# First mixture layer in column chunks across batches, and a global attention product with its operands swapped

## The chip, the cores and the metric

The kernel runs on one core of one Trainium2 chip. The metric is the device time of one execution in microseconds (us): the median over runs, on the same chip, of the kernel before and the kernel after the change.

## The reference, cut to what matters

Three layers follow each other. The first is attention over a global part of 32 positions and a local part of 512 positions, with a window of 32 on each side; its 544 positions by 512 features per batch are the input of a gated layer with a convolution over three positions, and this feeds a second layer that mixes each position with the one before it.

```python
# attention, 4 batches, 8 heads of 64
out_g = softmax(scale * q_g @ k_all.T) @ v_all          # 32 global rows, all 544 columns
out_l = softmax(window of q_l @ k_l.T, and k_g) @ v
x = concat(out_g, out_l)                                # (4, 544, 512)
# first MoE
h = relu(x @ w_in)                                      # 512 -> 1024
conv = sum(conv_w[k] * shifted(h, k - 1) for k in 0, 1, 2)   # zero at both ends of a batch
x = (h * sigmoid(conv)) @ w_out                         # 1024 -> 512
# second MoE
xk = mu_k * x + (1 - mu_k) * x_prev;  xr = mu_r * x + (1 - mu_r) * x_prev
out = sigmoid(xr @ w_r) * (relu(xk @ w_k) ** 2 @ w_v)
```

## The kernel before, in words

Everything is built by a planner. `add` declares a task with an engine, a cost and buffers, and `Plan.schedule` chooses an order from costs, keys (due times) and a set of numbers at the top of the file; the instructions then stand on each engine's queue in that fixed order. Engines wait for each other by semaphores, so a late input holds everything that is queued behind it on its engine.

The attention works on 16 units, each a pair of heads of one batch (`attend`), and every second unit closes with the global rows of two units (`glob`). A unit's steps on PE (TensorE) are the scores `s`, two transposes `pe`, the products with v `o`, and a transpose `X`, which brings the result into columns. The global rows have the scores `sg`, transposes `peg`, and the value product `Xg` (`fpv`, L719), in which v is the stationary operand (64 columns) and 32 columns of probabilities stream. DVE (VectorE) masks and divides, ACT (ScalarE) exponentiates and copies. POOL (GpSimd) helps with both.

Every product of the two MoE layers is taken as three matmuls: high part by high part, high by low, low by high. The parts are made by a copy (`fh`) and a subtraction (`fl`). The first MoE (`dense`) runs batch by batch. `ph` is the product with w_in (L901) over 8 tiles of 128 features, `po` the product with w_out (L1002) over 4 tiles. The 544 positions of a batch are cut at 256 (`SPLIT`), so each weight tile is loaded for a matmul of 256 and for one of 288 columns. Between them `relu`, the convolution `c` (L936, L943), the sigmoid, the gate product (L952) and its high and low parts (`gh`, `gl`, L959, L964) run on ACT, DVE and POOL. The result goes to DRAM as `x2d`, one tile per batch.

The second MoE (`moe2`) reads `x2d` in chunks of 384, 384, 384, 512 and 512 positions. A chunk has the products `pk` (L1140, 8 tiles, weight stationary), `pr` (L1204) and `pv` (L1241). Per `pk` tile there follow a relu, a square (`sq`, L1161), a high part and a low part (`k2l`, L1173), on ACT, DVE and POOL. The weights arrive as 64-bit numbers and are narrowed on ACT, DVE and POOL; their high and low parts are made at L839 and L842.

Of the kernel before, what the change touches and what calls it, by code (L numbers as in the profile page):

```python
# [26 lines left out]
SPLIT = (0, 256, S)  # L27
SP1 = S + 1
TOK = B * S
CH = 512  # L30
# [17 lines left out]
XB = 8  # L48
T_START = 3024
STEP0 = 2060  # L50
T_DENSE = 158430
SLOT = 122790
LEAD = 618
GAP = 13519
GAP1 = 18152
STEPS_H = 6
E_BUFS = 4
H_FRAC = 0.271
LAG_TE = -1744
LAG_PV = 112946  # L60
LAG_G = 3584
# [5 lines left out]
LAG_TX = 69395  # L67
WINDOW = 108
FILL_MIN = 5374
FILL_MARGIN = 1592  # L70
FILL_START = 6
FILL_RATE = 0.834
PENALTY = 4
AHEAD = 2243
PHASES = (111983, 150041, 327818, 468472)
# [30 lines left out]
def first_col(f):  # L106

    return 32 * (f + f // 3)

# [238 lines left out]
ROWS = {"s": 128, "pv": 64, "te": 8, "tx": 8, "gt": 6, "gs": 16, "gpv": 96, "warm": 6}  # L348
# [52 lines left out]
def attn_moe_kernel(  # L401
# [26 lines left out]
    def skewed(ap):  # L428
# [6 lines left out]
        [dram.tile([P, SP1], F32, tag=f"x2d{b}_{m}", name=f"x2d{b}_{m}") for m in range(KT)]  # L435
        for b in range(B)
# [17 lines left out]
    ident = const.tile([P, P], F32, name="ident")  # L454
    mask = const.tile([P, 4, P], F32, name="mask")
# [5 lines left out]
    make_identity(nc, ident)  # L461
    nc.gpsimd.memset(mask, 0.0)

# [58 lines left out]
    def attend(u):  # L522
# [89 lines left out]
        bx = bufs["x", u]  # L612

        def fh(copy):
            copy(bx[0].tile[:, SG:], bX.tile)

        def fl():
            nc.vector.tensor_sub(bx[1].tile[:, SG:], bX.tile, bx[0].tile[:, SG:].bitcast(F32))

        h = add("ACT", act(512), lambda: fh(nc.scalar.copy), deps=[tx, ev["xa", u]],  # L620
                use=[bX] + bx, name=f"xh{u}",
                alts=[("DVE", 600, lambda: fh(nc.vector.tensor_copy))])
        l = add("DVE", tt(512), fl, deps=[h], use=[bX] + bx, name=f"xl{u}")
        ev["x", u] += [h, l]

    def x_alloc(u):
        bufs["x", u] = [buf("x0"), buf("x1")]

        def fn():
            for i, b in enumerate(bufs["x", u]):  # L630
                alloc(b, [P, S], F32R, f"x{i}_{u}")

        ev["xa", u] = add("-", 0, fn, take=bufs["x", u], name=f"xa{u}")
        ev["x", u] = []
# [5 lines left out]
    def glob(u):  # L640
# [70 lines left out]
        def fpv():  # L711
            X = alloc(bt[2], [P, 2, SG], F32, f"Xg{u}")
            eT = bT.tile
            for z in range(2):
                v = bufs["v", u - 1 + z].tile
                for n, (_, f, rows) in enumerate(gchunks):
                    for a in range(2):
                        c = SG * (2 * z + a)
# [14 lines left out]
        for q in range(2):  # L733
# [4 lines left out]
        pvd = add("PE", 1522, fpv, deps=evs + [ev["v", u - 1], ev["v", u], ev["xa", u - 1], ev["xa", u]], take=[bt[2]],  # L738
                  use=[bT, bufs["v", u - 1], bufs["v", u]], key=kt + 2000, name=f"gpv{u}")
        for z in range(2):  # L740
            uu = u - 1 + z
            bx = bufs["x", uu]

            def fh(uu=uu, z=z, bx=bx):
                nc.scalar.copy(bx[0].tile[:, 0:SG], bt[2].tile[:, z])

            def fl(z=z, bx=bx):
                nc.vector.tensor_sub(
                    bx[1].tile[:, 0:SG], bt[2].tile[:, z], bx[0].tile[:, 0:SG].bitcast(F32)
                )  # L750

            hh = add("ACT", 78, fh, deps=[pvd, ev["xa", uu]], use=[bt[2]] + bx, name=f"gxh{uu}")
            ll = add("DVE", 102, fl, deps=[hh], use=[bt[2]] + bx, name=f"gxl{uu}")
            ev["x", uu] += [hh, ll]
# [58 lines left out]
    def split_weights(nm, src, nt, ncol, pool, tag, rings, after=(), early=None, st=WST, pad=0):  # L813
        w = {}

        def falloc():
            w["hi"] = pool().tile([P, nt, ncol], F32R, tag=tag + "_hi", name=nm + "_hi")
            lo = pool().tile([P, nt * ncol + pad], F32R, tag=tag + "_lo", name=nm + "_lo")
            w["lo"] = lo[:, : nt * ncol].rearrange("p (k c) -> p k c", k=nt)
# [40 lines left out]
    h_cost = 12 * (mmr(256) + mmr(288))  # L860
    o_cost = 2 * h_cost

    def d_key(b, pos):
        hp = FT * h_cost
        t0 = T_DENSE + SLOT * b
        if b == B - 1:
            return t0 + pos
        if pos < hp:
            return t0 + SLOT * H_FRAC * pos / hp
        return t0 + SLOT * (H_FRAC + (1 - H_FRAC) * (pos - hp) / hp)  # L870

# [11 lines left out]
    def dense(b):  # L883
        gates = {}
        pairs = [(buf("gh"), buf("gl")) for _ in range(FT // 2)]
        for m in range(FT):
            bh, bc = buf("h"), buf("c")
            relu = []
            for hf in range(2):
                s0, s1 = SPLIT[hf], SPLIT[hf + 1]  # L890
                bp = buf("mm")

                def part(q, bp=bp, m=m, s0=s0, s1=s1, hf=hf):
                    if q == 0:
                        alloc(bp, [P, 288], F32, f"ph{b}_{m}_{hf}")
                        warm(bp.tile)
                    pm = bp.tile[:, : s1 - s0]
                    for k in (2 * q, 2 * q + 1):
                        xh, xl = (z.tile for z in bufs["x", NP * b + k])
                        for n, (w, x) in enumerate(((win["hi"], xh), (win["hi"], xl), (win["lo"], xh))):  # L900
                            nc.tensor.matmul(  # L901
                                pm, lhsT=w[:, k, P * m : P * (m + 1)], rhs=x[:, s0:s1],
                                start=(k == 0 and n == 0), stop=(k == KT - 1 and n == 2),
                            )

                pos = m * h_cost + hf * h_cost / 2
                cost = 6 * mmr(s1 - s0)
                c0 = P * m // WST * WST
                deps = [
                    [d for k in (2 * q, 2 * q + 1) for d in ev["x", NP * b + k] + win_done[k, c0]]  # L910
                    for q in range(2)
                ]
                use = [[z for k in (2 * q, 2 * q + 1) for z in bufs["x", NP * b + k]] for q in range(2)]
                last = mm_group(f"H{b}_{m}_{hf}", bp, 2, part, deps,
                                [d_key(b, pos), d_key(b, pos + cost)], cost, use, s1 - s0)
                ev["H", b, m, hf] = last

                def fr(e, bp=bp, bh=bh, s0=s0, s1=s1, hf=hf, m=m):
                    if hf == 0:
                        h = alloc(bh, [P, S + 2], F32, f"h{b}_{m}")  # L920
                        nc.gpsimd.memset(h[:, 0:1], 0.0)
                        nc.gpsimd.memset(h[:, S + 1 : S + 2], 0.0)
                    o, i = bh.tile[:, 1 + s0 : 1 + s1], bp.tile[:, : s1 - s0]
                    if e is nc.scalar:
                        e.activation(o, i, AF.Relu)
                    else:
                        e.tensor_scalar(o, i, 0.0, None, op0=ALU.max)  # L927

                relu.append(add("ACT", act(s1 - s0), lambda fr=fr: fr(nc.scalar), deps=[last] + relu[-1:], take=[bh] if hf == 0 else [],
                                use=[bp] + ([bh] if hf else []), name=f"relu{b}_{m}_{hf}",  # L930
                                alts=[("DVE", tt(s1 - s0), lambda fr=fr: fr(nc.vector))]))

            def fc0(e, bh=bh, bc=bc, m=m):
                c, h, w = alloc(bc, [P, S], F32, f"c{b}_{m}"), bh.tile, convw[:, m : m + 1]
                if e is nc.scalar:
                    e.activation(c, h[:, 0:S], AF.Copy, scale=w)  # L936
                elif e is nc.vector:
                    e.tensor_scalar(c, h[:, 0:S], w, None, op0=ALU.mult)
                else:
                    e.tensor_scalar(c, h[:, 0:S], w, 1.0, op0=ALU.mult, op1=ALU.mult)  # L940

            def fc(e, k, bh=bh, bc=bc, m=m):
                e.scalar_tensor_tensor(  # L943
                    bc.tile, bh.tile[:, k : k + S], convw[:, FT * k + m : FT * k + m + 1], bc.tile,
# [3 lines left out]
            def fs(bc=bc):  # L948
                nc.scalar.activation(bc.tile, bc.tile, AF.Sigmoid)

            def fg(e, bc=bc, bh=bh):
                e.tensor_mul(bc.tile, bc.tile, bh.tile[:, 1 : S + 1])  # L952
# [439 lines left out]
```

## Time and profile before

| what | us |
|---|---|
| median of 3 runs (lowest to highest) | 545.34 (543.71 to 545.44) |
| the profiled execution, its own time | 543.37 |
| its span, first to last instruction | 541.5 |
| PE busy | 524.4 |
| DVE busy | 337.4 |
| ACT busy | 265.3 |
| POOL busy | 96.3 |

The profile is of one execution. Busy time of PE counts overlapping matmuls once. The pace of a stream of matmuls is better read from the chain of waits, where a piece has a length and a count. DVE, ACT and POOL show the length of each instruction, which can overlap the next by a little.

### The profile page before, as it was taken

How to read it: one execution, taken by the hardware profiler on the slowest of the kernel's cores; microseconds unless marked ns; L12 is line 12 of the kernel's file. 1: busy time of each engine (PE TensorE's matmuls, PEld its weight loads, DVE VectorE, ACT ScalarE, POOL GpSimd, SP SyncE). 2: the span in 40 equal slices, each digit the busy share in tenths (PEclk: the TensorE clock that was granted, in tenths of full speed). 3: DMA queues.
4: the chain of work that ended last, by engine and by line, in shares of the span. 5: the costliest groups of instructions: out<-in, count | busy, mean ns of one | idle time of the engine just before them, and what ended most of it. 6: DMA issues, size and time to landing. Idle time of an engine off the chain costs nothing.

```text
span 541.5 us, 13485 instructions
## 1 busy us (share of the span) xinstructions
PE 524.4 (97%) x5400; PEld 473.2 (87%) x5400; DVE 337.4 (62%) x914; ACT 265.3 (49%) x605; POOL 96.3 (18%) x241
## 2 busy tenths in 40 slices
PE   7699998999999999999999999999999999999997
PEld 6578977899999899999999998998998888888887
DVE  3597499814974469624799899599499497210001
ACT  4799999946664688843994884001001001004300
POOL 3257695601101000000000210000000000007500
PEclk9899999999999999999999999999999999999999
DMA  8969926755537520101336643103101100010001
GB/s 301 369 192 383 365 70 227 274 187 167 182 102 227 189 94 16 56 33 53 119 105 208 189 137 86 42 0 98 39 2 58 40 0 1 26 53 1 0 21 59
DMA packets 40510, 64.57 MB, mean 119 GB/s; under 512 B 4864, under 2 KB 30208, under 8 KB 40448
## 3 DMA queue, kind: packets, MB, share of 16 engines
q1 hardware_dynamic: 38144, 59.26, 33.0%
q10 hardware_dynamic: 2304, 4.47, 2.2%
q8 instruction: 42, 0.69, 0.5%
q14 instruction: 20, 0.16, 0.1%
HBM read 51.64 MB, written 12.07 MB: 118 GB/s over the span
## 4 chain that ended last, share of the span: by engine, by line
PE 84%; DMA 7%; DVE 4%; ACT 2%; issue 1%; POOL 1%; SPq 1%; POOLq 0%; ACTq 0%
PE pk L1140 18%; PE ph L901 17%; PE pv L1241 17%; PE po L1002 14%; PE pr L1204 9%; DMA win_0r<-in_moe_w_in_dram 3%; PE s L536 2%; DMA kT<-in_k_l_dram 2%; PE o L577 2%; PE pe L567 1%; PE Xg L719 1%; DVE c L943 1%; PE sg L660 1%; PE peg L704 1%; ACT e L558 1%
## 5 line engine op out<-in xcount | busy, mean ns | idle before, releaser
L901 PE MATMUL ph<-x,win_hi 128*128 128x256 f32 (+1 forms) x512 | 97.8, 290 | 1.0 <-DVE h L927 1.0
L901 PEld LDWEIGHTS ph<-x,win_hi 128*128 128x128 f32 x512 | 79.9, 188 | 1.4 <-DVE h L927 1.2
L1002 PE MATMUL po<-gh,wout_hi 128*128 128x288 f32 (+1 forms) x256 | 76.1, 297 | 0.0
L1002 PE MATMUL po<-gl,wout_hi 128*128 128x288 f32 (+1 forms) x256 | 73.8, 288 | 0.0
L1002 PE MATMUL po<-gh,wout_lo 128*128 128x288 f32 (+1 forms) x256 | 73.4, 287 | 0.0
L901 PE MATMUL ph<-x,win_lo 128*128 128x288 f32 (+1 forms) x256 | 73.3, 286 | 0.0
L1254 DVE TENSOR_TENSOR robuf<-pv,robuf 128x512 f32<-128x512 f32 (+1 forms) x18 | 11.9, 661 | 87.5 <-PE pv L1241 83.0
L1140 PE MATMUL pk<-xkh,wkk_lo 128*128 128x384 f32 (+1 forms) x160 | 57.6, 360 | 0.0
L1140 PE MATMUL pk<-xkh,wkk_hi 128*128 128x384 f32 (+1 forms) x160 | 57.6, 360 | 0.0
L1140 PE MATMUL pk<-xkl,wkk_hi 128*128 128x384 f32 (+1 forms) x160 | 57.5, 359 | 0.0
L943 DVE SCALAR_TENSOR_TENSOR c<-h,convw,c 128x544 f32<-128x544 f32 x64 | 51.3, 820 | 9.6 <-ACT c L936 9.0
L1241 PE MATMUL pv<-wvv_hi,k2h 128*128 128x512 f32 (+1 forms) x144 | 54.4, 378 | 0.0
L1241 PE MATMUL pv<-wvv_lo,k2h 128*128 128x512 f32 (+1 forms) x144 | 54.4, 377 | 0.0
L1241 PE MATMUL pv<-wvv_hi,k2l 128*128 128x512 f32 (+1 forms) x144 | 54.3, 377 | 0.0
L1002 PEld LDWEIGHTS po<-gh,wout_hi 128*128 128x128 f32 x256 | 48.2, 188 | 0.6 <-issue 0.2
L901 PEld LDWEIGHTS ph<-x,win_lo 128*128 128x128 f32 x256 | 48.2, 188 | 0.0
L1002 PEld LDWEIGHTS po<-gl,wout_hi 128*128 128x128 f32 x256 | 48.2, 188 | 0.0
L1002 PEld LDWEIGHTS po<-gh,wout_lo 128*128 128x128 f32 x256 | 48.2, 188 | 0.0
L558 ACT ACTIVATE e<-e 128x128 f32<-128x128 f32 x128 | 40.3, 395 | 7.2 <-DVE e L551 7.0
L1204 PE MATMUL pr<-wrr_hi,xrbuf 128*128 128x512 f32 x136 | 43.5, 395 | 0.0
L551 DVE CUSTOM_DVE_ANT_0 e<-s,mask 128x128 f32<-128x128 f32 x128 | 28.3, 285 | 16.6 <-PE s L536 16.6
L1219 ACT ACTIVATE robuf<-pr 128x512 f32<-128x512 f32 x17 | 10.2, 598 | 56.9 <-PE pr L1204 54.7
(170 smaller groups left out, 1045.7 us busy)
## 6 DMA issues: line engine op xcount, KB each, us to landing
v<-in_v_l_dram SPq DMA_DIRECT2D x16, 910.0 KB, 8.0
kT<-in_k_l_dram SPq DMA_DIRECT2D x16, 336.0 KB, 5.6
qT<-in_q_l_dram SPq DMA_DIRECT2D x16, 288.0 KB, 5.1
x2d<-xo ACTq DMA_DIRECT2D x16, 272.5 KB, 2.8
out_dram<-robuf SPq DMA_DIRECT2D x16, 256.0 KB, 2.0
wout_0r<-in_moe_w_out_dram SPq DMA_DIRECT2D x8, 256.0 KB, 5.9
wkk<-wkkd SPq DMA_DIRECT2D x8, 256.0 KB, 3.0
wout_0r<-in_moe_w_out_dram SPq DMA_DIRECT2D x8, 255.8 KB, 6.1
```

The lines of the kernel that those rows point to most:

```text
L536: nc.tensor.matmul(s[a][32 * j : 32 * j + 32, i], lhsT=qT[rows[a], q : q + 32], rhs=kT[rows[a], c : c + P], start=(i == 0), stop=True, ski ...
L551: nc.vector.tensor_tensor_reduce(out=e[:, P * i : P * (i + 1)], in0=bs[a].tile[:, i], in1=mask[:, i], scale=-SCALE, scalar=HUGE, op0=ALU.a ...
L558: nc.scalar.activation(be.tile[:, P * i : P * (i + 1)], be.tile[:, P * i : P * (i + 1)], AF.Exp, bias=be.tile[:, SL + i : SL + i + 1], sca ...
L577: nc.tensor.matmul(o[32 * j : 32 * j + 32, i], lhsT=bt.tile[:, i, 32 * j : 32 * j + 32], rhs=v[:, a, first_block(4 * i + j)], start=(i == ...
L901: nc.tensor.matmul(pm, lhsT=w[:, k, P * m : P * (m + 1)], rhs=x[:, s0:s1], start=(k == 0 and n == 0), stop=(k == KT - 1 and n == 2),)
L943: e.scalar_tensor_tensor(bc.tile, bh.tile[:, k : k + S], convw[:, FT * k + m : FT * k + m + 1], bc.tile, op0=ALU.mult, op1=ALU.add,)
L1002: nc.tensor.matmul(pm, lhsT=w[:, k, P * m : P * (m + 1)], rhs=g[:, k % 2, s0:s1], start=(k == 0 and n == 0), stop=(k == FT - 1 and n == 2),)
L1140: nc.tensor.matmul(bp.tile[:, :n], lhsT=w[:, k, P * m : P * (m + 1)], rhs=x[:, :n], start=(k == 0 and i == 0), stop=(k == KT - 1 and i == 2),)
L1204: nc.tensor.matmul(bp.tile, lhsT=x[:, P * j : P * (j + 1)], rhs=w[:, k], start=(k == 0 and i == 0), stop=(k == KT - 1 and i == 2),)
L1219: nc.scalar.activation(r(), bp.tile, AF.Sigmoid)
L1241: nc.tensor.matmul(bp.tile, lhsT=x, rhs=w[:, k, c0:c1], start=(k == 0 and i == 0), stop=(k == FT - 1 and i == 2),)
L1254: nc.vector.tensor_mul(o()[:, c0:c1], bp.tile, r()[:, c0:c1])
```

## The change

The first MoE no longer runs batch by batch. Its columns are those of all four batches side by side, with one zero column between batches (4 x 545 = 2180), in five chunks of 480, 480, 480, 480 and 260. `ph` takes two more columns than its chunk, for the convolution's neighbours (482 and 262), and a weight tile is loaded once per chunk. The relu, the convolution and the gate run on the whole width. A unit's attention result goes to one or two chunks (`windows`), and POOL writes the zero columns.

The global value product is swapped: 32 columns of probabilities are stationary and 64 columns of v stream, into four column groups. Its result lies in rows, so a copy to SBUF (`fcopy`) and one matmul with a folded identity (`fturn`) bring it into columns.

The second MoE has chunks of 384 five times and 256 once, and the padding of one weight tile is gone. All numbers of the planner are new.

```diff
-SPLIT = (0, 256, S)
+GAPPED = B * (S + 1)
+CW = (480, 480, 480, 480, 260)
+NC = len(CW)
+CA = tuple(sum(CW[:c]) for c in range(NC + 1))
...
-XB = 8
-T_START = 3024
+XB = 10
+T_START = -32416
...
-DVE_BIAS = (1653, 4571, -7537, -14876, 20094)
-ACT_BIAS = (882, 4155, -17189, -12831, -3045)
-POOL_BIAS = (480, 9104, -6750, -14338, -21669)
+DVE_BIAS = (425, 13181, -112, 8785, 3254)
+ACT_BIAS = (-8199, -1203, -224, -20768, -16631)
+POOL_BIAS = (24870, -34502, -354, -10831, 5828)
...
+def windows(b, t0, t1):
+    lo, hi = (S + 1) * b + t0, (S + 1) * b + t1
+    found = []
+    for c in range(NC):
+        p0, p1 = max(lo, CA[c] - 1), min(hi, CA[c + 1] + 1)
+        if p0 < p1:
+            found.append((c, p0 - CA[c] + 1, p0 - lo + t0, p1 - p0))
+    return found
...
         def fpv():
-            X = alloc(bt[2], [P, 2, SG], F32, f"Xg{u}")
+            X = alloc(bt[2], [P, P + 2 * SG], F32, f"Xg{u}")
...
-                        nc.tensor.matmul(
-                            X[D * a : D * (a + 1), z], lhsT=v[:rows, a, f, :D], rhs=eT[:rows, n, c : c + SG],
-                            start=(n == 0), stop=(n == 5), skip_group_check=True,
-                        )
+                            nc.tensor.matmul(
+                                X[at : at + SG, D * a : D * (a + 1)], lhsT=eT[:rows, n, c : c + SG],
+                                rhs=bufs["v", u - 1 + z].tile[:rows, a, f, :D], start=(m == 0 and a == 0), stop=True,
+                                skip_group_check=True,
+                            )
+
+        def fcopy(copy):
+            copy(be.tile[:, :P], bt[2].tile[:, :P])
+
+        def fturn():
+            nc.tensor.matmul(
+                bt[2].tile[:, P:], lhsT=be.tile[:, :P], rhs=fold, start=True, stop=True, skip_group_check=True,
+            )
...
     def dense(b):
-            for hf in range(2):
-                s0, s1 = SPLIT[hf], SPLIT[hf + 1]
-                    pm = bp.tile[:, : s1 - s0]
-                        xh, xl = (z.tile for z in bufs["x", NP * b + k])
-                                pm, lhsT=w[:, k, P * m : P * (m + 1)], rhs=x[:, s0:s1],
+                    xh, xl = (z.tile for z in bufs["x", b, k])
+                            bp.tile[:, : w + 2], lhsT=wt[:, k, P * m : P * (m + 1)], rhs=x[:, : w + 2],
...
-                                pm, lhsT=w[:, k, P * m : P * (m + 1)], rhs=g[:, k % 2, s0:s1],
+                            bp.tile[:, :w], lhsT=wt[:, k, P * m : P * (m + 1)], rhs=g[:, k % 2, :w],
...
-    widths = (384, 384, 384, 512, 512)
+    widths = (384, 384, 384, 384, 384, 256)
...
-    for b in range(B):
+    for b in range(NC):
         if b + 1 < B:
             attention(b + 1)
         dense(b)
```

The next rows are PE's queue around the second global value product, which lies in the first tiles of the first MoE. `ph` with a number of tile and half is the product with w_in, `Xg` the value product, `egT` the probabilities, `v` the values, `x` the attention's result. Before:

```order
L901 MATMUL ph_1_1_893<-x_0_160,win_hi 128x288
L901 MATMUL ph_1_1_893<-x_0_161,win_hi 128x288
L901 MATMUL ph_1_1_893<-x_0_160,win_lo 128x288
L901 MATMUL ph_1_1_893<-x_1_162,win_hi 128x288
L901 MATMUL ph_1_1_893<-x_1_163,win_hi 128x288
L901 MATMUL ph_1_1_893<-x_1_162,win_lo 128x288
L719 MATMUL Xg_909<-egT_857,v_307 64x32 x12
L719 MATMUL Xg_909<-egT_857,v_385 64x32 x12
L567 MATMUL pe_0_944<-ident,e_0_782 128x128 x4
```

With the change (the last two of 24 rows of the swapped product stand first):

```order
L757 MATMUL Xg_973<-v_370,egT_879 32x64
L757 MATMUL Xg_973<-v_414,egT_879 32x64
L602 MATMUL o_0_1010<-v_679,eT_0_922 32x65 x16
L602 MATMUL o_1_1031<-v_679,eT_1_999 32x65 x16
L633 MATMUL X_1055<-ident,xn_917 128x128 x4
L955 MATMUL ph_1_1062<-x_0_0_168,win_hi 128x482
L955 MATMUL ph_1_1062<-x_0_0_170,win_hi 128x482
L955 MATMUL ph_1_1062<-x_0_0_168,win_lo 128x482
L955 MATMUL ph_1_1062<-x_0_1_176,win_hi 128x482
L955 MATMUL ph_1_1062<-x_0_1_178,win_hi 128x482
L955 MATMUL ph_1_1062<-x_0_1_176,win_lo 128x482
L767 MATMUL Xg_973<-fold,eg_722 128x64
```

The same 24 matmuls of the value product now write 32 rows by 64 columns, six matmuls of 482 columns stand for twelve of 256 and 288, and the folding matmul stands behind other work of PE.

The other place is POOL in the second MoE. Before, it has no such work until the last chunk of 512; `robuf` is the square, `k2l` its low part, `wvv` the last weight. Before:

```order
L780 MEMSET wvv_0m 128x256
L780 MEMSET wvv_256m 128x256
L1161 TENSOR_TENSOR robuf<-robuf 128x512
L1173 TENSOR_TENSOR k2l_0_6720<-robuf,k2h_0_6718 128x512
L1161 TENSOR_TENSOR robuf<-robuf 128x512
```

With the change, a piece between two chunks (`d` is the difference to the position before, `xkl` and `xrbuf` low parts of the mixed inputs of the next chunk):

```order
L1208 TENSOR_TENSOR robuf<-robuf 128x384 x2
L1220 TENSOR_TENSOR k2l_6_5321<-robuf,k2h_6_5315 128x384 x2
L1124 TENSOR_TENSOR d_1_5339<-x_2_1_5046 128x385
L1124 TENSOR_TENSOR d_2_5341<-x_2_2_5088 128x385
L1124 TENSOR_TENSOR d_3_5354<-x_2_3_5136 128x385
L1150 TENSOR_TENSOR xkl_0_5379<-xt2xk_5299,xkh_0_5304 128x384
L1150 TENSOR_TENSOR xkl_1_5394<-xt2xk_5351,xkh_1_5362 128x384
L1150 TENSOR_TENSOR xkl_2_5409<-xt2xk_5364,xkh_2_5377 128x384
L1150 TENSOR_TENSOR xkl_3_5424<-xt2xk_5374,xkh_3_5382 128x384
L1164 TENSOR_TENSOR xrbuf<-xt2xr_5306,xrbuf 128x384
```

POOL had 8 squares and 8 low parts of 512 columns there. It now has 29 squares and 30 low parts of 384, and besides them 20 differences, 19 low parts of xk and 16 of xr.

## Rows read from the trace of the kernel before

**Rows 1.** The page: span, busiest engine, slices of its busy share and granted clock.

```profile
span 541.5 us, 13485 instructions
PE 524.4 (97%) x5400; PEld 473.2 (87%) x5400; DVE 337.4 (62%) x914; ACT 265.3 (49%) x605; POOL 96.3 (18%) x241
PE   7699998999999999999999999999999999999997
PEclk9899999999999999999999999999999999999999
```

**Rows 2.** Busy time by stage: PE, PEld, DVE, ACT, POOL (instructions), clock, DMA share, GB/s.

```profile
0.00:37.00 37.00, 28.69 (x707) 22.62 (x708) 20.98 (x119) 24.20 (x65) 12.91 (x41) 0.95 0.85 293
37.00:105.00 68.00, 63.16 (x1231) 56.24 (x1229) 53.88 (x189) 64.88 (x152) 47.47 (x72) 1.00 0.76 269
105.00:255.00 150.00, 149.04 (x1967) 144.07 (x1968) 86.08 (x258) 96.66 (x226) 12.06 (x88) 1.00 0.37 118
255.00:303.20 48.20, 48.20 (x385) 48.20 (x385) 42.12 (x72) 35.31 (x72) 2.46 (x16) 1.00 0.50 150
303.20:541.50 238.30, 235.29 (x1116) 202.10 (x1115) 134.32 (x279) 44.24 (x93) 21.35 (x26) 1.00 0.13 44
```

**Rows 3.** The chain that ended last, PE's pieces: start us, length us, line, matmuls.

```profile
37.02 0.72 PE ph L901 x6
38.17 0.79 PE ph L901 x6
...
74.31 0.59 PE o L577 x32
...
75.49 0.44 PE pe L567 x4
...
132.74 1.52 PE Xg L719 x48
134.26 1.50 PE o L577 x96
...
254.97 24.12 PE ph L901 x192
279.09 24.11 PE po L1002 x192
303.20 16.67 PE pk L1140 x96
...
427.58 22.24 PE pk L1140 x96
...
461.02 21.78 PE pv L1241 x96
```

**Rows 4.** PE's instructions in order of time, two early waits: start, length, instructions, [idle before].

```profile
18.53 1.07 PE L536 MATMUL s<-kT,qT 64*32 64x128 f32 x54 [1.28 <-DMA kT<-in_k_l_dram]
21.81 0.43 PE L536 MATMUL s<-kT,qT 64*32 64x128 f32 x10 [2.21 <-issue]
```

**Rows 5.** Groups by line and shape: busy us, mean ns of one, idle before.

```profile
L964 POOL TENSOR_TENSOR gl<-c,gh 128x544 fp32r<-128x544 f32 x8 | 11.1, 1403 | 0.0
L1173 POOL TENSOR_TENSOR k2l<-robuf,k2h 128x512 fp32r<-128x512 f32 x8 | 10.3, 1290 | 4.4 <-ACT k2h L1168 4.4
L1161 POOL TENSOR_TENSOR robuf<-robuf 128x512 f32<-128x512 f32 x8 | 8.3, 1042 | 164.0 <-ACT robuf L1156 164.0
L952 DVE TENSOR_TENSOR c<-c,h 128x544 f32<-128x544 f32 x24 | 17.2, 719 | 2.4 <-ACT c L949 2.0
L1158 DVE TENSOR_SCALAR robuf<-pk 128x384 f32<-128x384 f32 x16 | 8.9, 557 | 2.8 <-PE pk L1140 2.8
L842 DVE TENSOR_TENSOR wkk_lo<-wkk,wkk_hi 128x512 fp32r<-128x512 f32 x8 | 5.4, 682 | 2.7 <-DMA wkk<-wkkd 2.7
```

More of the change, by code (lines that the diff above doesn't have):

```diff
@@ L434, in attn_moe_kernel @@
     x2d = [
[L435 to L436 removed]
+        [dram.tile([P, CW[c] + (c == 0)], F32, tag=f"x2d{c}_{m}", name=f"x2d{c}_{m}") for m in range(KT)]
+        for c in range(NC)
     ]
@@ L454, in attn_moe_kernel @@
     ident = const.tile([P, P], F32, name="ident")
+    fold = const.tile([P, 64], F32, name="fold")
+    zero = const.tile([P, 1], F32, name="zero")
     mask = const.tile([P, 4, P], F32, name="mask")
@@ new lines, in dense, with part @@
+            bp = buf("mm")
+            def part(q, bp=bp, m=m):
+                if q == 0:
+                    alloc(bp, [P, CH0], F32, f"ph{b}_{m}")
+                    warm(bp.tile)
+                for k in (2 * q, 2 * q + 1):
+                    xh, xl = (z.tile for z in bufs["x", b, k])
+                    for n, (wt, x) in enumerate(((win["hi"], xh), (win["hi"], xl), (win["lo"], xh))):
+                        nc.tensor.matmul(
+                            bp.tile[:, : w + 2], lhsT=wt[:, k, P * m : P * (m + 1)], rhs=x[:, : w + 2],
+                            start=(k == 0 and n == 0), stop=(k == KT - 1 and n == 2),
+                        )
@@ new lines, in dense, with part @@
+            bp = buf("mm")
+            def part(q, bp=bp, m=m):
+                if q == 0:
+                    alloc(bp, [P, CH0], F32, f"po{b}_{m}")
+                    warm(bp.tile)
+                gh, gl = (z.tile for z in pairs[q])
+                for k in (2 * q, 2 * q + 1):
+                    for n, (wt, g) in enumerate(((wout["hi"], gh), (wout["hi"], gl), (wout["lo"], gh))):
+                        nc.tensor.matmul(
+                            bp.tile[:, :w], lhsT=wt[:, k, P * m : P * (m + 1)], rhs=g[:, k % 2, :w],
+                            start=(k == 0 and n == 0), stop=(k == FT - 1 and n == 2),
+                        )
@@ new lines, in dense, with fo @@
+            pos = base + m * o_cost
+            cost = o_cost / 4
+            deps = [gates[2 * q] + gates[2 * q + 1] + wout_done[2 * q, 0] + wout_done[2 * q + 1, 0]
+                    for q in range(4)]
+            last = mm_group(f"O{b}_{m}", bp, 4, part, deps,
+                            [d_key(b, pos + q * cost) for q in range(4)], cost,
+                            [list(pairs[q]) for q in range(4)], w)
+            ev["O", b, m] = last
+            lead = int(b == 0)
+            def fo(copy, bp=bp, bo=bo, m=m):
+                xo = alloc(bo, [P, XO], F32, f"xo{b}_{m}")
+                if lead:
+                    nc.gpsimd.memset(xo[:, 0:1], 0.0)
+                copy(xo[:, lead : lead + w], bp.tile[:, :w])
@@ L1025, in dense @@
+            evs = [add("ACT", act(w), lambda fo=fo: fo(nc.scalar.copy), deps=[last], take=[bo],
+                       use=[bp], name=f"oe{b}_{m}",
+                       alts=[("DVE", tt(w), lambda fo=fo: fo(nc.vector.tensor_copy))])]
             ev["relu", b] = relu[-1]
             ev["x2", b, m] = add(
-                "AQ", 900, lambda bo=bo, m=m: load_to(eng=nc.scalar, out=x2d[b][m], in_=bo.tile),
+                "AQ", 900, lambda bo=bo, m=m: load_to(eng=nc.scalar, out=x2d[b][m], in_=bo.tile[:, : lead + w]),
@@ L1064, in chunk @@
             wd = n + len(segs)
+            first = (S + 1) * b0 + off - 1
+            spans = pieces(first, first + wd)
+            if first < 0:
+                spans[0] = (0, first, spans[0][2])
             xk, xkb, xr = [], [], []
```

307 lines of the change are left out of this document (143 added, 164 removed).

## The prediction

> **What bounds the kernel now.** I read the page first. PE is busy 524.4 of 541.5 us, and the 40 slices show it full from the third slice on at the full granted clock; no other engine passes 62% [rows 1]. So the question is what PE has to do, and where it waits. The busy time by stage answers the second [rows 2]. In the first 37 us PE is idle for 37 - 28.69 = 8.31 us, between 37 and 105 for 4.84, between 105 and 255 for 0.96, in the 48.2 us of the last batch of the first MoE for none. The 3.0 us that are missing after 303.2 are the end of the kernel, where the last product has been written and only DVE and a store follow. The early waits are inputs that arrive late: a load of k, and a wait for which the profile shows no cause [rows 4]. Between 37 and 105 ACT is the fuller engine, 64.88 of 68 us, with DVE at 53.88.
>
> What PE has to do is read from the chain of waits, where a piece of a stream has a length and a number of matmuls [rows 3]. From 255 on the chain is PE alone, product after product. A change is thus worth what it takes off PE's stream, less what it adds in waits.
>
> **First MoE, wider matmuls.** Six of 256 columns take 0.72 us, six of 288 take 0.79, and the last batch's 192 of both kinds take 24.12 us for ph and 24.11 for po [rows 3]. Four batches make 4 x 48.23 = 192.9 us for 1536 matmuls. Now there are 768 of 480 or 482 columns and 192 of 260 or 262, 960 in all. The columns streamed are nearly the same (2180 against 2176, and 2 more per chunk for ph), so only the part of a matmul that does not grow with its width can be saved. The trace has no 480. From below, 384 columns take 16.67 / 96 = 0.1736 us in pk. From above, 512 take 22.24 / 96 = 0.2317 in pk and 21.78 / 96 = 0.2269 in pv [rows 3]. On the line to pv, 481 columns come out at 0.2140, on the line to pk at 0.2177. I take 0.2158, the middle, since pk has the same form and pv the lower price. The 260 are priced like the 256, with a little more for their columns, at 0.1215. That gives 768 x 0.2158 + 192 x 0.1215 = 165.7 + 23.3 = 189.0, a gain of 3.9 us, and by the ends 5.2 and 2.4.
>
> The page "TensorE: Matmul & The Clock Gate" of the Trainium skill, section "Back-to-back issue gap", gives N / 2.4 + 2.5 ns for warm matmuls, a fixed part of 2.5 ns. The rows above disagree: 120 ns at 256 columns, where that rule has 109. By the rule the 576 matmuls that go would save 1.4 us in place of 3.9.
>
> **Global value product.** 48 recorded matmuls, 64 columns stationary and 32 streaming, take 1.52 us; there are eight such groups, 12.2 us [rows 3]. The trace has no swapped form of it, but `o` has the same one: 32 columns stationary, 65 streaming, into four column groups. There 96 take 1.50 us [rows 3], so 48 would take 0.75. The other end is that nothing is gained, 1.52. I take 0.75, whose row differs by one column: a gain of 8 x 0.77 = 6.2 us.
>
> The turn back adds a matmul of 64 columns per group. Four transposes of 128 take 0.44, 0.11 each, and the first matmuls after another kind cost some 0.09 more: 32 of `o` alone take 0.59 against 0.50 in a row [rows 3]. So 0.2 each, 1.6 us in all, with 0.9 (the step alone) and 3 as ends. It waits for the copy before it. In PE's order work of `o`, `X` and `ph` stands between in nearly all groups, so I cost the wait at nothing; without that cover it would be a copy and two hand-overs, well under 1 us per group.
>
> **Smaller terms on PE.** The new order has eight filler matmuls in front of other work, each like a transpose: 0.11 x 8 = 0.9 us. The second MoE turns two pk chunks of 512 into two of 384 and one of 256: 2 x 16.67 + 96 x 0.12 - 2 x 22.24 = +0.4. Its pr and pv matmuls are the same in number and width.
>
> **Off PE.** A relu now reads 482 columns from one bank, and an `x` result is cut into two pieces in many units, all beside PE. POOL writes 48 zero columns instead of the 64 at the edges of h. The loads of weights and units move bytes as before; in SP's queue one more k and v stand in front of the last w_out, and one more q and k in front of the first w_in. I cost this at nothing, since PE has these units' attention to do in the meantime; if that cover fails, it lands in the waits of the first 105 us.
>
> **Sum.** -3.9 - 6.2 + 1.6 + 0.9 + 0.4 = -7.2 us, with PE's waits as they were. The profiled execution took 543.37, which becomes 536.2. It stands 2.0 below the median of 545.34, and that becomes **538.1**.
>
> **Rivals.**
>
> *Early waits go too.* ACT is at 95% between 37 and 105 [rows 2], and the new order gives DVE ten of its 32 wide relus and eleven of its first convolution steps. If all idle time of PE between 37 and 255 went, 5.8 us, the time would be 532.3. Against it: part of that time is loads, which are no smaller.
>
> *DVE takes ACT's place.* By the counts in the queues DVE gets 7 more relus, 11 first convolution steps, 13 more gate products and 12 more low parts at smaller width, 8 low parts of w_out and about 20 high parts. At 0.70 us for a wide read from PSUM, 0.63 for a product of 480 and 0.68 for a weight tile [rows 5] that is at most 39 us on top of the 203 that DVE is busy up to 303.2 [rows 2]: 82% of the new stretch. It also has to finish attention within the first three chunks, where before it had three whole batches. If PE's idle time between 37 and 255 doubles, the time is 543.9, a tie by what can be measured.
>
> *POOL bounds the second MoE, slower than before.* The new place of the squares and low parts is POOL. Scaled from 512 columns a square takes 0.78 us and a low part 0.97 [rows 5], 1.75 for a tile that takes PE 12 x 0.1736 = 2.08. With differences and the parts of the next chunk POOL has about 20 of 41 us per chunk. It decides when the pair passes 2.08. At half as much again it would be 2.63, and six tiles in each of five chunks would cost 5 x 6 x 0.55 = 16.5 us: 554.6. For it: before, DVE did nearly nothing beside POOL in this work, and now DVE works next to it. Against it: in the first MoE, beside a busy DVE, a low part took 1403 ns at 544 columns, the same per column as in the quiet last chunk [rows 5]. The page "GPSIMD Engine Reference" of the Trainium skill, section "Specifications", says that POOL shares its SBUF interfaces with DVE, with contention for DVE instructions that have two SBUF inputs; these rows show no such price.
>
> *The change does not do what it says.* The swap gains nothing and 480 columns cost the upper price: -2.4 + 1.6 + 0.9 + 0.4 = +0.5, 545.8. Against it is the row of `o`.
>
> **How the numbers follow.** The forecast, PE's sum with waits within 3 us of before, has 0.60. The early waits that go have 0.14, DVE in ACT's place 0.13, POOL 0.07, no effect 0.06. The range reaches from 532 (the first rival) to 545 (just past the second) and leaves out POOL and the tie. A difference of 0.3%, 1.6 us, is about the least that a measurement of this kernel can tell from none. Faster by more than that are the forecast, the first rival and 0.06 of the second, where waits grow by less: 0.80. The tie is the case of no effect and 0.04 of the second: 0.10. Slower are POOL and 0.03 of the second, where waits more than double: 0.10.
>
> **What would show it.** In the changed profile: ph and po at 0.214 to 0.218 us per matmul of 480 in the chain, the swapped product at 0.75 us per group, the fold under 0.3, the second MoE within 1 us of 235 us from its first pk to its last pv, and PE's idle time before it between 11 and 17 us. The prediction is wrong if ph or po wait for DVE inside the first three chunks for more than 6 us in all, if pk or pv wait for POOL, or if the swapped product stays near 1.5 us.

## The result, and the profile after

The change made the kernel slower: 550.47 us (median of 4 runs, 547.88 to 550.83) against 544.53 for the kernel before on the same chip, a ratio of 1.010 (95% interval 1.006 to 1.014). Forecast were 538.1 us, range 532 to 545, and "faster" with 0.80. The profiled execution has a span of 548.8 us where that of before had 541.5 [rows 1].

The page of the changed kernel:

```profile
span 548.8 us, 12707 instructions
PE 525.0 (96%) x4952; PEld 453.8 (83%) x4952; DVE 321.5 (59%) x893; ACT 295.0 (54%) x659; POOL 177.4 (32%) x312
PE   6679997999899999999999999999999999999997
PEclk9799999999999999999999999999999999999999
```

PE has 448 matmuls fewer and is as busy as before, 525.0 against 524.4 us. So its work did not shrink by the 7.2 us of the sum, and 7 us of span came on top. Busy time by stage, cut where the first `ph` begins, at 105, at 255 and shortly before the first `pk`, which begins at 306.75 (after the bounds PE, PEld, DVE, ACT, POOL, granted clock, DMA share, GB/s):

```profile
0.00:44.15 44.15, 31.94 (x789) 25.77 (x789) 22.64 (x136) 27.45 (x77) 16.14 (x63) 0.88 0.91 319
44.15:105.00 60.85, 56.65 (x606) 46.92 (x604) 53.05 (x148) 49.85 (x110) 19.22 (x40) 0.97 0.68 227
105.00:255.00 150.00, 146.22 (x2030) 121.88 (x2029) 112.06 (x374) 102.56 (x223) 21.93 (x63) 1.00 0.41 133
255.00:306.10 51.10, 51.10 (x318) 47.21 (x317) 41.39 (x85) 29.26 (x63) 1.24 (x4) 1.00 0.32 99
306.10:548.80 242.70, 239.12 (x1219) 212.05 (x1217) 92.36 (x153) 85.93 (x189) 118.84 (x142) 1.00 0.16 48
```

Against [rows 2]: the first `ph` comes 7 us later, with 12.21 us of PE idle ahead of it instead of 8.31; the middle stage has 3.78 us of idle instead of 0.96; the second MoE, from its first `pk` on, takes 3 us more of PE (238.47 us against 235.46), though its matmuls stream as many columns. The granted clock is below 1 in the first two stages, 0.88 and 0.97; before it was 0.95 in the first only. The early figures vary by some 2 us from profile to profile: rows_aligned, below, has the changed kernel's order on every engine, and there the first `ph` comes at 41.52, with 10.3 us of idle ahead of it.

PE's pieces in the chain that ended last (start, length, product, line, matmuls):

```profile
45.72 0.81 PE Xg L757 x48
...
242.84 19.70 PE ph L955 x90
262.54 20.96 PE po L1044 x96
...
391.46 16.87 PE pk L1187 x96
408.33 8.39 PE pr L1251 x36
416.72 16.73 PE pv L1288 x72
```

The swap does what was forecast, 0.81 for 1.52 [rows 3]. But `ph` takes 0.2189 us per matmul of 482 columns and `po` 0.2183 per 480, above the upper end of 0.2177. And `pv`, which the change does not touch, went from 0.2269 [rows 3] to 0.2323.

PE's time by product, summed in the trace from each matmul's start to the next one's start, with idle time taken out (number of matmuls in brackets; fillers are matmuls whose result nobody reads):

| us | before | after | forecast of the difference |
|---|---|---|---|
| ph and po | 197.3 | 199.4 | -3.9 |
| of these next to other work or a wait, at full clock | 10.4 (48) | 20.8 (67) | none |
| of these at the lower clock | 0 | 3.4 (8) | none |
| global value product, fold | 12.2, 0 | 6.1, 1.8 | -6.2, +1.6 |
| pk | 94.8 | 95.9 | +0.4 |
| pr, pv | 140.4 | 142.3 | 0 |
| fillers | 0 | 2.1 | +0.9 |
| rest of attention, start | 79.4 | 77.2 | 0 |
| sum | 524.1 | 524.7 | -7.2 |
| idle between matmuls | 13.1 | 18.8 | 0 |

Three things went wrong, then: what a matmul costs, how often the stream of `ph` and `po` is cut, and where PE waits. The second is in the rows on matmuls next to other work: the first or last of a run takes about 0.3 us where 0.22 is the pace, at a granted clock of 1.00. The new order cuts `ph` and `po` into 49 runs, the old one into 36, and the surplus over the pace is 6.1 us instead of 4.4.

The largest waits, from PE's instructions in order of time ([idle before, and what ended it]):

```profile
14.75 3.77 PE L561 MATMUL s<-kT,qT 64*32 64x128 f32 x128 [4.12 <-DMA kT<-in_k_l_dram]
...
27.68 0.75 PE L757 MATMUL Xg<-v,egT 96*32 96x64 f32 x35 [1.95 <-issue]
...
40.28 2.24 PE L561 MATMUL s<-kT,qT 64*32 64x128 f32 x64 [2.24 <-DMA kT<-in_k_l_dram]
...
93.30 1.38 PE L445 MATMUL peg<-ident 128*128 128x128 f32 x10 [3.81 <-ACT eT L595]
...
95.34 0.60 PE L1044 MATMUL po<-gl,wout_hi 128*128 128x480 f32 x1
95.74 0.60 PE L1044 MATMUL po<-gh,wout_lo 128*128 128x480 f32 x1
```

Behind the wait at 93.30, `po` starts every 0.40 us instead of every 0.22: the lower of the two clock levels, 1.2 GHz in place of 2.4, for eight matmuls. The stage view of PE (bounds, length, busy, granted clock, DMA share, GB/s) has 0.50 there:

```profile
94.80:98.10 3.30, 3.30 (x10) 0.50 0.34 115
```

The chain says what PE waited for there:

```profile
79.80 4.45 DMA wout_0r<-in_moe_w_out_dram
...
84.35 0.04 ACT wout_0m L838
84.39 0.77 issue
85.16 1.28 ACT L713
...
87.50 1.03 ACT wout_hi L891 x2
88.53 0.49 ACT gh L1005
89.02 0.02 issue
89.04 1.28 ACT L995
...
92.77 0.49 ACT eT L595
```

The last part of w_out is issued at 79.4 us (before, the last such issues began at 59.10); the longest wait of SP's queue ahead of it, 8.2 us, ends when DVE has narrowed an earlier part. The narrowing of the last part stands in ACT's queue ahead of the exponentials of a global group, and two table loads and the gate's copies follow before `eT`, for which PE waits.

### The profile page after: what moved, and what is told of

Read it like the earlier page. It is cut to its first block, busy times and chain, and to the rows that moved or that the text cites. A ratio compares the mean times of both kernels' runs of the same rounds, so it can differ in the third digit from the quotient of the medians.

```text
span 548.8 us, 12707 instructions
## 1 busy us (share of the span) xinstructions
PE 525.0 (96%) x4952; PEld 453.8 (83%) x4952; DVE 321.5 (59%) x893; ACT 295.0 (54%) x659; POOL 177.4 (32%) x312
## 4 chain that ended last, share of the span: by engine, by line
PE 76%; DVE 7%; POOL 4%; DMA 4%; ACT 4%; issue 3%; SPq 1%; ACTq 0%; DVEq 0%; POOLq 0%
PE ph L955 15%; PE pv L1288 14%; PE po L1044 14%; PE pk L1187 14%; PE pr L1251 7%; DMA kT<-in_k_l_dram 3%; PE o L602 2%; PE s L561 2%; PE pe L592 2%; DVE c L989 2%; POOL wvv_lo L894 1%; PE Xg L757 1%; PE X L633 1%; PE peg L740 1%; POOL k2l L1220 1%
## 5 line engine op out<-in xcount | busy, mean ns | idle before, releaser
L955 PE MATMUL ph<-x,win_hi 128*128 128x482 f32 (+1 forms) x320 | 90.9, 369 | 0.0
L1044 PE MATMUL po<-gh,wout_hi 128*128 128x480 f32 (+1 forms) x160 | 60.6, 379 | 1.5 <-DVE e L576 1.5
L1044 PE MATMUL po<-gl,wout_hi 128*128 128x480 f32 (+1 forms) x160 | 58.5, 366 | 0.0
L1044 PE MATMUL po<-gh,wout_lo 128*128 128x480 f32 (+1 forms) x160 | 58.3, 365 | 0.0
L955 PE MATMUL ph<-x,win_lo 128*128 128x482 f32 (+1 forms) x160 | 57.9, 362 | 0.0
L989 DVE SCALAR_TENSOR_TENSOR c<-h,convw,c 128x480 f32<-128x480 f32 (+1 forms) x80 | 52.9, 681 | 6.7 <-ACT c L982 6.4
L1187 PEld LDWEIGHTS pk<-xkl,wkk_hi 128*128 128x128 f32 x192 | 36.1, 188 | 1.0 <-POOL xkl L1150 0.6
L1187 PEld LDWEIGHTS pk<-xkh,wkk_hi 128*128 128x128 f32 x192 | 36.1, 188 | 0.2
L1187 PEld LDWEIGHTS pk<-xkh,wkk_lo 128*128 128x128 f32 x192 | 36.0, 188 | 0.0
L1215 ACT CAST k2h<-robuf 128x384 fp32r<-128x384 f32 (+1 forms) x48 | 23.6, 494 | 21.9 <-POOL robuf L1208 13.2
```

Of the source, the lines that this page charges most:

```text
L955: nc.tensor.matmul(bp.tile[:, : w + 2], lhsT=wt[:, k, P * m : P * (m + 1)], rhs=x[:, : w + 2], start=(k == 0 and n == 0), stop=(k == KT - ...
L989: e.scalar_tensor_tensor(bc.tile[:, :w], bh.tile[:, k : k + w], convw[:, FT * k + m : FT * k + m + 1], bc.tile[:, :w], op0=ALU.mult, op1=A ...
L1044: nc.tensor.matmul(bp.tile[:, :w], lhsT=wt[:, k, P * m : P * (m + 1)], rhs=g[:, k % 2, :w], start=(k == 0 and n == 0), stop=(k == FT - 1 a ...
L1187: nc.tensor.matmul(bp.tile[:, :n], lhsT=w[:, k, P * m : P * (m + 1)], rhs=x[:, :n], start=(k == 0 and i == 0), stop=(k == KT - 1 and i == 2),)
L1215: copy(bg[0].tile[:, m % 2, :n], ks()[:, :n])
```

## The experiments

Three questions: what sets the pace of a wide matmul, what brings the waits, and what the change is worth without them. Each run was timed against the kernel before on the same chip; since that median moves (542.25 to 544.53), kernels are compared by their ratio to it.

| run | median us | ratio to before (95%) |
|---|---|---|
| rows_aligned | 549.04 | 1.011 (1.008 to 1.014) |
| before_shifted | 542.77 | 1.001 (0.999 to 1.003) |
| before_w2_aligned | 542.43 | 1.0005 (0.998 to 1.003) |
| before_w2_256 | 541.70 | 0.997 (0.995 to 1.000) |
| rows_256 | 545.98 | 1.006 (1.004 to 1.008) |
| before_swapped | 549.87 | 1.013 (1.010 to 1.016) |
| third_unit_first | 550.25 | 1.013 (1.011 to 1.016) |
| renumbered | 542.70 | 0.9997 (0.998 to 1.001) |
| renumbered_256 | 538.96 | 0.994 (0.992 to 0.996) |
| renumbered_256_b | 536.36 | 0.986 (0.982 to 0.989) |
| chunks_448 | 535.98 | 0.986 (0.983 to 0.990) |

### The pace of a matmul: absolute addresses

**rows_aligned**

```diff
-    zero = const.tile([P, 1], F32, name="zero")
+    zero = const.tile([P, 32], F32, name="zero")
...
-                    alloc(bg[0], [P, 2, XW], F32R, f"gh{b}_{m}")
+                    alloc(bg[0], [P, 2, XW - 2], F32R, f"gh{b}_{m}")
```

> Edit: the changed kernel, with the small zero tile widened to 128 bytes per partition, which puts the weights of both MoE layers that lie on the left of SBUF (w_in, w_out, w_v) on addresses that are a multiple of 128, and with the gate tiles 480 instead of 482 columns wide, which does the same for the rows of gh, gl, k2h, k2l. No instruction moves on any engine. Theory A (the pace of wide matmuls hangs on where their operands begin in SBUF): po of 480 columns falls from 219 to 213 or 214 ns, pv of 512 from 232 to 227, ph, whose x tiles stay scattered, to between 213 and 219; 384 matmuls of each, so 4 to 6 us less than the changed kernel, 544.5 to 546.5. Theory B (the pace is set by what the other engines do at the same time, and the new order keeps them busier): po 219, pv 232, time as the changed kernel, 550.

**before_shifted**

```diff
+    zero = const.tile([P, 1], F32, name="zero")
     mask = const.tile([P, 4, P], F32, name="mask")
...
+    nc.gpsimd.memset(zero, 0.0)
```

> Edit: the kernel before, with an unused tile of 32 bytes per partition ahead of the constants, so that w_in, w_out, w_v and all x, gate and k2 tiles begin 32 bytes later; nothing else differs, and no instruction moves. Theory A: pv of 512 columns goes from 227 to 232 ns as in the changed kernel, 384 of them make 2 us more, 546.5; ph and po of 256 and 288 columns stay within 1 or 2 ns, as the 260 of the changed kernel did. Theory B: pv stays at 227 and the time at 544.5.

**before_w2_aligned**

```diff
-[att_done], early["wrr"], pad=8)
+[att_done], early["wrr"], pad=24)
```

> Edit: the kernel before, with the padding of the low part of w_r grown from 8 to 24 columns, which puts w_k and w_r on a multiple of 128 bytes (before, they lie 64 bytes behind one); no instruction moves. Theory A: pr falls from 233 to 227 ns (204 matmuls, -1.3 us), pk of 512 from 232 to 227 (192 matmuls, -1.1 us), pk of 384 stays at 174: 542.1. Theory B: nothing moves, 544.5.

The memset is one instruction more on POOL. All three went against theory A as it stood. The first two show `pv` in the chain, aligned and at 0.232 in rows_aligned, shifted and still at 0.227 in before_shifted:

```profile
407.53 8.41 PE pr L1251 x36
415.94 16.70 PE pv L1288 x72
```

```profile
330.75 16.35 PE pv L1243 x72
```

In before_w2_aligned `pr` stays at 0.233 (8.40 for 36) and `pk` of 512 comes down by a little, to 0.2279 in the last chunk (21.88 for 96). Theory B does not hold either: in the changed kernel, the starts of `pv` lie 232 ns apart both in the 123 places where DVE, ACT and POOL all rest and in some 165 where POOL works throughout. The Trainium skill says in "SBUF — State Buffer", section "SBUF: two separate sides", that PE never waits for another engine at SBUF's ports; this trace agrees, with 232 ns in both.

One pattern was left. Wherever 512 columns took 227 ns, the row that streams and the weight row that is loaded for the next matmul began a multiple of 256 bytes apart; wherever they took 231 to 234, all or half of them did not. (Where a tile begins is read from the addresses in the built program.)

### The pace of a matmul: the distance of its operands

**rows_256**

```diff
-    zero = const.tile([P, 1], F32, name="zero")
+    zero = xp.tile([P, 32], F32, name="zero")
...
-                    alloc(bg[0], [P, 2, XW], F32R, f"gh{b}_{m}")
+                    alloc(bg[0], [P, 2, CH0], F32R, f"gh{b}_{m}")
...
-[att_done], early["wrr"])
+[att_done], early["wrr"], pad=56)
```

> Edit: the changed kernel with addresses alone moved. The zero tile lies behind the weights, the rows of the gate tiles are 2048 bytes apart instead of 1928, and w_k and w_r move down, so that in po, pr and pv the rows of both operands begin at the same place modulo 256 bytes. No instruction moves. The last four runs left one pattern: 227 ns for 512 columns wherever the two operands lay a multiple of 256 bytes apart, 232 to 234 elsewhere, whatever their absolute place. Theory A2 (this distance sets the pace): pv 227 (384 matmuls, -2 us), pr 227 (204, -1.3), po of 480 at 213 to 214 (384, -2), ph as it was, 219: 545 us. If the pattern was chance: pv 232, po 218, 550.

The chain of rows_256:

```profile
260.67 20.81 PE po L1045 x96
...
405.44 8.16 PE pr L1252 x36
413.60 16.32 PE pv L1289 x72
```

`pr` falls from 8.39 to 8.16 (0.2267 each) and `pv` from 16.73 to 16.32 (0.2267), both as forecast, with no instruction moved. `po` comes down to 0.2168, not to 0.2135. Summed over the trace, `pv` gains 1.9 us, `pr` 1.2 and `po` 1.5. The ratio goes from 1.010 to 1.006, with intervals that overlap; on the same chip third_unit_first, which keeps the changed kernel's addresses, took 549.11 to 550.74 us, and rows_256 544.42 to 546.72.

**before_w2_256**

```diff
-[att_done], early["wrr"], pad=8)
+[att_done], early["wrr"], pad=56)
```

> Edit: the kernel before, with the padding of the low part of w_r grown from 8 to 56 columns, which puts w_k and w_r a multiple of 256 bytes from w_v's place and from the mixed inputs; no instruction moves. Theory A2: pr goes from 233 to 227 (204 matmuls, -1.2 us); pk of 512, whose x rows are 2176 bytes apart and so lie at 0 or 128, goes from 232.5 to 228 or 229 (192, -0.8); 540 to 541, 2 us under the kernel before. Otherwise no change.

```profile
403.10 8.17 PE pr L1204 x36
...
427.59 22.17 PE pk L1140 x96
```

In the kernel before, too, `pr` falls to 0.227 by a padding alone. `pk` of 512 stays at 0.231, with x rows that lie at both 0 and 128: this half of the expectation failed. The time is 0.3% lower, at the edge of what can be told.

So the distance decides for whole streams of `pv` and `pr`: `pv` is at 0.227 in the nine kernels where all its rows keep it and at 0.232 in the four where they don't (the changed kernel, rows_aligned, third_unit_first, renumbered), and `pr` is at 0.227 in the five that place w_r so and at 0.233 elsewhere. It is not shown for matmuls of 480, and matmul by matmul it does not hold. In rows_aligned the 192 matmuls of `pv` that keep the distance take 230.9 ns on average and the other 187, among which they stand, 232.7; in before_w2_256 the 63 of `pk` that keep it take 231.8 and the other 127 230.6. Only in the last chunk of before_w2_aligned, where 79 of 95 keep it, do these reach 226.6. What the distance does inside the chip stays open.

### The waits

**before_swapped** (the new functions are those of the change)

```diff
-        pvd = add("PE", 1522, fpv, deps=evs + [...
+        pvd = add("PE", 705, fpv, deps=evs + [ev["v", u - 1], ev["v", u]], take=[bt[2]],
...
+        pvd = add("PE", 180, fturn, deps=[cp, ev["xa", u - 1], ev["xa", u]], use=[bt[2], be], key=kt + 2500, name=f"gy{u}")
```

> Edit: the kernel before with the swapped global value product alone (with its copy and its folding matmul); chunks, numbers of the planner and second MoE as before. The sum of the prediction: 8 groups at 0.76 less, 8 folds at 0.2 more, so 4.3 to 4.6 us less than before, about 540, if PE's waits stay as they were. Rival: what the planner makes of the new tasks brings waits of its own into the first 105 us, as in the changed kernel, where idle time of PE grew by 5.7 us: 545 or more.

The rival held, and by more than it said. With before's chunks and before's numbers, the swap alone gives a kernel as slow as the whole change. Stages of PE alone (bounds, length, busy, granted clock, DMA share, GB/s):

```profile
0.00:45.00 45.00, 32.05 (x777) 0.86 0.93 324
45.00:105.00 60.00, 55.64 (x833) 0.96 0.54 185
105.00:255.00 150.00, 146.59 (x2184) 1.00 0.44 140
```

Summed over the trace, the product and its fold take 8.8 us where the product alone took 12.2, so the swap saves 3.3; but idle between matmuls rose from 13.1 to 19.5, and the clock fell in the first two stages (before, cut at the same bounds, it was 0.96 and 1.00). Part of the idle time is the swapped product's own, for its inputs come late from ACT:

```profile
39.88 0.53 PE L723 MATMUL Xg<-v,egT 96*32 96x64 f32 x20 [1.93 <-ACT egT L711]
41.42 0.65 PE L723 MATMUL Xg<-v,egT 96*32 96x64 f32 x28 [1.00 <-ACT egT L711]
...
43.73 0.69 PE L733 MATMUL Xg<-fold,eg 128*128 128x64 f32 x2 [1.02 <-ACT eg L730]
```

A planner that is given other tasks writes another order everywhere. That before's numbers do not fit the new tasks is the likely reading; the swap alone with numbers fitted to it was not run.

**third_unit_first**

```diff
-    for t in plan.schedule():
+    order = plan.schedule()
+    named = {t.name: t for t in order}
+    for nm in ("ldq2", "ldk2"):
+        order.remove(named[nm])
+        order.insert(order.index(named["ldv0"]), named[nm])
+    for t in order:
```

> Edit: the changed kernel with the third unit's loads of q and k put ahead of the first two loads of v in SP's queue, as in the kernel before; nothing else moves on any engine. Theory (the order of the first loads makes the early waits): the scores of the third unit start near 10 us instead of 14.75 and the wait of 4.12 us falls below 1.5; the first ph starts 2 to 3 us earlier than 44.15; time 547.5 to 548.5. Rival (the first 40 us are bound by the bytes to load, whatever their order): the wait comes back at o, which needs v, or at the next k, and the time stays at 550.

```profile
10.50 1.16 PE L561 MATMUL s<-kT,qT 64*32 64x128 f32 x64
16.59 1.96 PE L561 MATMUL s<-kT,qT 64*32 64x128 f32 x64 [4.93 <-DMA kT<-in_k_l_dram]
```

The third unit's scores start at 10.50, as the theory had it, and the fourth unit's then wait 4.93 us for their own k, which now lands behind both loads of v. The time is unchanged: the rival held. One load put forward only moves the wait to the next one, with DMA at 0.9 of its time in this stage.

**renumbered** (the numbers come from a search over the planner's own estimate)

```diff
-T_START = -32416
-STEP0 = 7098
-T_DENSE = 24497
+T_START = -112209
+STEP0 = 512
+T_DENSE = 99947
...
-DVE_BIAS = (425, 13181, -112, 8785, 3254)
+DVE_BIAS = (9004, 31132, -112, 35551, 2393)
```

> Edit: the changed kernel with other numbers for the planner alone (keys, lags, biases, filler rules); the same tasks, chunks, tiles and swap, in another order. Theory (the chunks and the swap are worth what was forecast, and the order that the new numbers gave costs it): PE's idle time falls from 18.8 to 13 us or less, its time at the lower clock in ph and po from 8 us too much to 4 or less, fillers from 2.1 to under 0.5; together 11 us less than the changed kernel, 539 to 541. Rival (chunks of 480 with a batch of attention between them bring these waits in any order, because DVE and ACT have to finish attention within three chunks): idle stays above 17 us and the time at 547 or more.

```profile
0.00:45.00 45.00, 30.34 (x852) 0.92 0.86 297
45.00:105.00 60.00, 57.31 (x794) 1.00 0.70 238
105.00:255.00 150.00, 148.47 (x1788) 1.00 0.45 144
```

The order alone takes back the whole loss: ratio 0.9997 against 1.010, the same tasks, tiles and chunks. But neither half of the expectation came: the time is above 539 to 541, and idle time fell only from 18.8 to 17.2 us, which is the rival's figure without the rival's time. Behind 45 us the waits shrink (PE idle 2.7 us between 45 and 105, 1.5 between 105 and 255; in the changed kernel 4.2 and 3.8), but the first 45 us have 14.7 us of idle, more than the 12.2 of the changed kernel and the 8.4 of before. Most of the gain is PE's own time, 520.1 us for 525.0: fillers fell from 2.1 to 0.6 us, `ph` and `po` from 199.4 to 196.5, cut into 41 runs instead of 49 and none of them at the lower clock. The figure of 8 us too much at the lower clock, in the expectation, counted the matmuls next to other work; at the lower clock there were 3.4 us in all.

**renumbered_256** joins the edits of rows_256 and renumbered.

> Edit: the two edits of rows_256 and renumbered together. If both hold, their gains add, since one shortens matmuls where PE never waits and the other takes away waits: 534 to 536, 7 to 9 us below the kernel before. If only the order holds, 539 to 541; if only the addresses, 545.

Ratio 0.994, against 0.9997 for the order alone and 1.006 for the addresses alone: 1.6% under the changed kernel where the two parts give 1.0 and 0.4. Within what can be told the gains add; the time expected was 3 us too low, with 15.4 us of idle between matmuls still there, 12.6 of them in the first 45 us.

**renumbered_256_b** takes a further set of numbers on the addresses of rows_256.

> Edit: as renumbered_256, with one more set of numbers for the planner, in whose order fewer steps of attention stand ahead of the first ph. If PE's waits in the first 45 us come from the order of the early steps, they fall from 12 us to under 10, and the time to 535 to 537. If they are bound by the bytes of the early loads, they stay at 12 to 14 and the time at 538 to 540.

The two halves of the expectation came apart. The time is that of the first, 536.4, but idle between matmuls in the first 45 us is 12.9 us, as the second had it. What fell lies later: 0.6 us of idle behind 45 us, where renumbered_256 has 2.8. So three orders, among them one with fewer steps of attention ahead of the first `ph`, did not move the early waits. Loaded bytes may be part of it: the kernel before has moved 10.8 MB when its first `ph` starts, the changed one 14.1 and this one 13.3. They can't be all of it, for chunks_448, in yet another order, has moved 14.7 MB and has 9.0 us. The waits that end on "issue" are another part (see the last section). How much each is worth stays open.

**chunks_448**

```diff
-CW = (480, 480, 480, 480, 260)
+CW = (446, 446, 446, 446, 396)
...
-T_START = -32416
...
```

> Edit: the addresses as in rows_256, but chunks of 446, 446, 446, 446 and 396, so that ph streams 448 columns and x, gate and k2 rows are 1792 bytes apart, a multiple of 256; the numbers of the planner are new again. Question: why po of 480 came down to 217 only, where 512 came down to 227. Theory W (the pace is best only where a matmul's own length is a multiple of 64 columns too): the line through pv (120 at 256, 227 at 512) gives 200 ns at 448, 199.2 at 446 and 178 at 396; ph of 448 reaches 200, po of 446, whose rows are as well placed, stays 3 to 6 above its 199.2, and pk of 384 stays at 174. Rival (rows are enough, and 480 was short of the line for another reason): ph and po of 448 and 446 both at 199 to 201. Rival 2 (neither): both at 203 to 206. Time 536 to 540, depending on the waits that the new order brings.

```profile
223.35 19.46 PE ph L956 x96
242.81 19.21 PE po L1045 x96
262.02 17.15 PE ph L956 x96
279.17 17.27 PE po L1045 x96
...
337.63 16.66 PE pk L1188 x96
354.30 8.20 PE pr L1252 x36
362.50 16.32 PE pv L1289 x72
```

Theory W fell: `po` of 446 is the one near the line (0.2001 against 0.1992), `ph` of 448 the one above it (0.2027 against 0.2000). `pk` of 384, with all rows a multiple of 256 bytes apart, takes 0.1735, with starts 173 to 174 ns apart. What keeps `ph` of 448 and `po` of 480 some 3 ns above the line stays open. The kernel takes 536.0 us, 1.4% under the kernel before and 2.4% under the changed one, and holds the swap, the wide chunks and the second MoE in 384s.

## Why the prediction was wrong

**The step that failed first: "with PE's waits as they were".** It carried the sign. The row of the table on idle grew by 5.7 us. The lower clock behind the wait at 93.30 took 1.6 more, eight matmuls in 3.4 us where at 0.219 they would take 1.75, and the finer interleaving of `ph` and `po` with other work 1.7, a term that the sum does not have, though it uses the 0.09 us of a first matmul for the fold. That the order causes the loss as a whole is shown by renumbered, which changes nothing else and brings the ratio from 1.010 to 0.9997. The forecast gain is not there even so: PE's own time is 4.3 us below that of before, not 7.2, and 4.1 us more of idle eat it. The prediction costed the shifts in SP's queue at nothing, "since PE has these units' attention to do in the meantime". That cover does not exist: the waits at 14.75 and 40.28 are the attention's own scores waiting for k. The text did name what follows if the cover fails, but gave it no chance beyond a part of the second rival. Of w_out it counted one more k and v in front of the last part, and not that the last three parts wait for buffers until 74.9 us. That the narrowing of w_out stands ahead of the exponentials in ACT's queue could have been seen in the new order.

**The price of 480 columns** was mis-sized. 0.2158 was taken, 0.2183 to 0.2189 measured. At that price and 0.122 for the last chunk the part is worth -1.6 us, not -3.9. The two rows that were taken as ends, `pk` and `pv` of 512, differed for a reason that the prediction did not ask for. The rows now show it for `pv`: the distance of the operands in SBUF.

**"Its pr and pv matmuls are the same in number and width"** was true and not enough: the new constants and gate rows moved their operands, and `pv` went up by 2.0 us. rows_256 gives these back by addresses alone.

**The rule that the prediction took from the Trainium skill**, N / 2.4 + 2.5 ns ("TensorE: Matmul & The Clock Gate", section "Back-to-back issue gap"), is given there for an isolated matmul, and the prediction set it against a stream with a weight load for each. It is further off than the line that the prediction drew: 480 columns would take 202.5 ns by it, an estimate; measured were 218.

**Right:** the swap (-6.1 for -6.2), the fold (+1.8 for +1.6), `pk`'s new widths within 0.7. **Too low:** the fillers, +2.1 for +0.9: the eight are recorded as 16 matmuls, ten of which run behind the wait at 93.30 and not in it. **Not forecast:** the rest of attention took 2.2 us less, for which no run shows the reason.

**The rivals.** DVE did not take ACT's place: it is busy 229.1 us up to the first `pk`, where at most 242 were estimated, and the one wait of `po` that ends on it is 1.52 us, not 6. Nearly all idle time of the middle stage, 3.8 us, does end on DVE, but most of it lies in front of `peg` and `o`. POOL does not bound the second MoE: it is busy 118.84 of 242.7 us there, half of the stage as estimated, and only one wait of PE, of 0.24 us, ends on it. The case that came true, early waits that grow, had 0.03 as the tail of another rival. It should have been the rival on the other side.

## What to carry to other kernels

Where a planner or a scheduler writes the order, an edit of any task rewrites the whole order, and the sum of costs holds only for the order that it was made with. Read the new queues for what now stands ahead of a late input on each engine that copies or narrows, give "the waits grow" a chance of its own, and judge the edit after the order has been fitted to it. And when two rows of the same shape differ by 2%, ask what differs before taking them as ends: here, for `pv` and `pr`, it was where two tiles lay.

## What the runs showed of the hardware that was not expected

A stream of matmuls of 512 columns, each with its own weights, runs at 227 ns when in all of them the streaming row and the next weight row begin a multiple of 256 bytes apart within a partition (`pr` 8.39 to 8.16 us for 36, `pv` 16.73 to 16.32 for 72, by padding alone). Whether both rows begin at such a multiple themselves makes no difference: `pv` stays at 227 in before_shifted. Streams of which none or half keep the distance run at 230 to 234 ns, and matmuls that keep it gain nothing while they alternate with others that do not. For `pv`, it makes no difference whether the other engines work.

A matmul of `ph` or `po` next to work of another kind or a wait costs about 0.08 us more at a granted clock of 1.00 (0.30 for 0.22 at 480 columns). So the number of runs into which an order cuts a stream is a term of the sum.

Some of PE's waits have no releaser but "issue": 2.21 us in the kernel before [rows 4], 1.61 and 1.95 in the changed one. The packets of one DMA queue, q8, tell what they are. Before and after the change it has

```profile
q8 instruction: 42, 0.69, 0.5%
q8 instruction: 39, 0.64, 0.5%
```

which is one packet of 16 KB per some 256 instructions of PE and its weight loads (10800 and 9904). In the 13 profiles PE has 29 such waits of more than 0.6 us, and 28 of them end 1.2 to 1.5 us after a packet of q8 has landed; the wait of 2.21 us ends 1.52 us after the packet that landed at 20.29. PE waits for its own instructions, then; 24 of the 29 lie in the first 50 us, where DMA is at 0.9 of its time. That is read from the times alone: no run changed these loads. In renumbered these waits are 7.3 us, half of the idle time ahead of its first `ph`; in chunks_448 they are 2.0.
